# Stage 4 of a fused attention and MoE kernel: the last eight weight sums are moved into three gated waves

## Chip, cores and metric

One NeuronCore of a Trainium2 chip. The metric is the device time of one execution in microseconds (us); the time of a kernel is the median of its runs. All times inside an execution are counted from the start of the profiled span.

## What is computed

```
attn = softmax(cap * tanh(q k^T / sqrt(64) / cap)) v      4 x 12 heads, 448 x 64
x    = attn as 1792 x 768
h    = ((x w1) * (x w2)) w3 w_out                          d_ff 1024
g    = h w_in;  e = g * softmax(g);  c = layernorm(e) * g_ln
out  = c w_out2                                            1792 x 768
```

The three weights w3, w_out and w_in are multiplied together once ("fold"), so the middle of the chain is one 1024 x 1024 matrix.

## The kernel before

**Stages.** Attention and fold share the first half (to about 420 us). Stage 4 ("gated", to about 578 us) makes the products (x w1) * (x w2), 128 columns of d_ff ("block" f) at a time. Two more stages follow: the folded 1024 x 1024 matrix, then w_out2, in pairs of 128-row tiles (`seven`). All products are split into a high and a low fp32r part and take three matmuls (`THREE`). Some products are done with seven half-size products in place of eight (Strassen): in stage 4 the blocks 11, 13 and 14 (`SEVEN`, function `strassen`), in the two last stages all of them.

**Stage 4's end.** After two blocks of another order, the blocks come as 10, 11, 12, 13, 14, 15. Of these 10, 12 and 15 are plain (`products`, L700 to L729): 36 matmuls (L716) for each batch b, whose first half is copied by ScalarE (`a`, L720) and multiplied with the second by VectorE (`abs`, L724). A Strassen block has three PSUM banks u, v and y. Its product 3 adds to u only after VectorE has read u (L768), and the bank u is free for block 13 only after VectorE's last read of it (L774). p1 and p7 are copies by ScalarE (L751); L766, L768, L770, L771 and L774 are VectorE's sums with them, and their results are stored (L755).

**A block's weights.** Blocks from 10 on are read again from DRAM (`wt`, L446, 1.5 MB). For a Strassen block POOL then makes sums of the weights (L459 to L478, ten instructions: s3, s1, s2, s4), ScalarE casts each (L175) and VectorE subtracts (L176) to get the low part. Their buffers rotate (tag `cv`, two of them), so POOL's sixth step waits for VectorE's L176 of the first sum.

**Weight sums.** The two last stages also need Strassen sums of their weights. For each piece `plan_sums` reads four sub-blocks into one landing buffer (`ld`, two DMAs, L160), VectorE makes four differences in place (L590 to L593) and SP stores the result in two DMAs (L596). Kind "t" serves the fifth stage (eight pieces, `tw_dr`), kind "tg" the sixth (eight pieces of 128 x 4 x 192, `tg_dr`). There are `LANDS` = 3 landing buffers; the same three also take the first operands of the fifth stage (`ldab`, L162).

**Order of the work.** A list `ahead` holds all such work in the order in which it was added: an item is read up to three items ahead (`depth`), and goes through `rest` when it is its turn. An item has a `there` condition for its read and a `gate` for its turn. The program is then scheduled by a list scheduler; `tc.issue_after(x)` holds an instruction behind x in that schedule. Every engine and the SP queue run their instructions in program order. In the list before: block 13's read (`plan_again(NF + 5)`), then the eight "tg" pieces, then the reads of blocks 14 and 15, with no gate; the first difference of a "tg" piece stands behind `last_t`, an early instruction of stage 4.

```
    plan_again(NF + 5)
    some_sums("tg", G4, tg_dr, range(NF // 2), DM // 4)
    for f in range(NF + 6, 2 * NF):
        plan_again(f)
```

Of the kernel before, what the change touches and what calls it, by code (L numbers as in the profile page):

```python
# [10 lines left out]
F32 = mybir.dt.float32  # L11
# [3 lines left out]
ALU = mybir.AluOpType  # L15
# [8 lines left out]
DM = H * D  # L24
# [75 lines left out]
def attention_moe_solu(ctx: ExitStack, tc: tile.TileContext, q, k, v, cap, w12, w3t, wo, win, wout2, g_ln, out):  # L100
# [50 lines left out]
    def landing(i, src, n, kind):  # L151
        t = conv.tile([P, 2 * HALF], U32, tag="ld", bufs=LANDS, name=f"ld{i}")
        lands[i] = t[:, :n].bitcast(kind)
        dst = lands[i]
        if len(src.shape) == 3:
            dst = dst.rearrange("p (a b) -> p a b", a=src.shape[1])
        elif len(src.shape) == 4:
            dst = dst.rearrange("p (a b c) -> p a b c", a=src.shape[1], b=src.shape[2])
            for g in range(src.shape[1]):
                sync.dma_start(out=dst[:, g], in_=src[:, g])  # L160
            return
        loads[i] = sync.dma_start(out=dst, in_=src)  # L162
# [373 lines left out]
    def w3_slot(name):  # L536
        return w3p.tile([P, 2, HALF], F32R, tag="w3", bufs=W3, name=name)[:, :, :S]

    last_t = [None]

    def plan_t(part):

# [32 lines left out]
    def four(dr, i, part, n):  # L575

        return dr[i][:, :, :, part * n:(part + 1) * n]
# [1 line left out]
    W4 = w_dr.rearrange("(g i) p (h n) -> i p g h n", g=2, h=2)  # L579
    G4 = wg_dr.rearrange("(g i) h p n -> i p g h n", g=2)  # L580

    def plan_sums(kind, dr, t_dr, i_, part, n):

        i = len(ahead.items)

        def rest():
            b = lands.pop(i).rearrange("p (g h n) -> p g h n", g=2, h=2)
            b00, b01, b10, b11 = (b[:, g, h] for g in range(2) for h in range(2))
            with tc.issue_after(last_t[0].ins) if kind == "tg" or i_ >= NF // 4 else nullcontext():
                dve.tensor_tensor(b00, b01, b00, ALU.subtract)  # L590
            dve.tensor_tensor(b01, b11, b01, ALU.subtract)
            dve.tensor_tensor(b11, b11, b00, ALU.subtract)
            dve.tensor_tensor(b10, b10, b11, ALU.subtract)  # L593
            b = b.rearrange("p g h n -> p (g h) n")
            for m, two in enumerate((b[:, ::3], b[:, 1:3])):
                sync.dma_start(out=t_dr[2 * m:2 * m + 2, :, i_, part * n:(part + 1) * n].rearrange("t p n -> p t n"), in_=two)  # L596
        ahead.add((kind, i_, part), lambda: landing(i, four(dr, i_, part, n), 4 * n, F32), lambda: None, rest, None, lambda: "ws" in place)

    def block_src(m, part, dr, t_dr):

# [51 lines left out]
    def some_sums(kind, dr, t_dr, two, n):  # L652
        for i_ in two:
            for part in range(2):
                plan_sums(kind, dr, t_dr, i_, part, n)
# [8 lines left out]
        for part in range(2):  # L664
            plan_block(m, part)
    plan_again(NF + 5)
    some_sums("tg", G4, tg_dr, range(NF // 2), DM // 4)
    for f in range(NF + 6, 2 * NF):
        plan_again(f)
    for m in EARLY[2:]:  # L670
        for part in range(2):
            plan_block(m, part)
# [25 lines left out]
    def gated():  # L698
        pp = {}

        def products(f, b, cs):
            at_ = f - 2 if f in (NF, NF + 1) else f
            for i in range(2):
                if cs[0] == 0:
                    tag = "o" if "ws" in place and (i if b < 3 or f >= NF + 2 else f % 2) else "f"
                    if (f, b) == (2 * NF - 1, PASSES[1][0]):
                        pp["sc"] = ps.tile([P, 2, HALF], F32, tag=f"sc{f % 2}", name="ab_last") if i == 0 else pp["sc"]
                        pp[f, b, i] = pp["sc"][:, i]
                    else:
                        pp[f, b, i] = ps.tile([P, HALF], F32, tag=tag, bufs=2, name=f"ab{i}_{f}_{b}")  # L710
                for c in cs:
                    while not (ahead.upto(("w", at_, c // 2)) and ahead.upto(("x", b, c // 2))):
                        yield 0
                    w = wt[at_][:, :, columns(i, c)]
                    for m, (u, e) in enumerate(THREE):
                        pe.matmul(pp[f, b, i][:, :S], w[:, u], xs[b, c][:, e], start=(c == 0 and m == 0), stop=(c == NC - 1 and m == 2))  # L716
                        yield 189
                if cs[-1] == NC - 1 and i == 0:
                    pp["a"] = place["ab"].tile([P, S], F32, tag="a", bufs=2, name=f"a_{f}_{b}")
                    act.copy(pp["a"], pp[f, b, 0][:, :S])  # L720
            if cs[-1] < NC - 1:
                return
            ab = place["ab"].tile([P, S], F32, tag="ab", bufs=2, name=f"abs_{f}_{b}")
            dve.tensor_tensor(ab, pp[f, b, 1][:, :S], pp["a"], ALU.mult)  # L724
            sync.dma_start(out=ab_dr[block(f), :, b * S:(b + 1) * S], in_=ab)
            if f < NF - 2 and b == PASSES[0][0]:
                sync.dma_start(out=w12_dr[f], in_=raw(wt[f]))
            fin.add((f, b))
            ahead.loads()  # L729

        def strassen(f):
            b1, b2 = PASSES[1]
            x = {1: [xs[b1, c] for c in range(0, NC, 2)], 2: [xs[b1, c] for c in range(1, NC, 2)], 3: [xs[b2, c] for c in range(1, NC, 2)]}
            u, y = (ps.tile([P, HALF], F32, tag=g, bufs=2, name=f"{n}_{f}")[:, :S] for n, g in (("u", "f"), ("y", "o")))
            v = ps.tile([P, 2, HALF], F32, tag=f"sc{f % 2}", name=f"v_{f}")[:, 0, :S]
            need = {1: ("w", f, 0), 7: ("t", NC // 2 - 1), 6: ("w", f, 1), 4: ("t4", NC // 2 - 1), 3: ("w", f, 2)}

            def product(bank, m, first):
                while m in need and not ahead.upto(need[m]):
                    yield 0  # L740
                for k in range(NC // 2):
                    part = slice(k * P, (k + 1) * P)
                    a = wt[f].rearrange("p a (k n) -> p a k n", n=HALF)[:, :, k, {1: slice(0, P), 2: slice(P, 2 * P), 5: slice(2 * P, 3 * P), 4: slice(3 * P, HALF)}[m]] if m in (1, 2, 4, 5) else st_[f][:, :, (6, 7, 3).index(m), part]
                    o = x[m][k] if m < 4 else ts_[m, k]
                    for i, (h, e) in enumerate(THREE):
                        pe.matmul(bank, a[:, h], o[:, e], start=(first and k == 0 and i == 0), stop=(k == NC // 2 - 1 and i == 2), skip_group_check=not first)  # L746
                        yield 189

            def kept(bank, p, tag, name):
                k_ = p.tile([P, S], F32, tag=tag, bufs=2, name=f"{name}_{f}") if tag != "rb" else p.tile([P, 2, S], F32, tag=tag, name=f"{name}_{f}")[:, 0]  # L750
                act.copy(k_, bank)  # L751
                return k_

            def send(k_, b):
                sync.dma_start(out=ab_dr[block(f), :, b * S:(b + 1) * S], in_=k_)  # L755
                fin.add((f, b))
                ahead.loads()
            yield from product(u, 1, True)
            one = kept(u, place["ab"], "a", "p1")
            yield from product(v, 7, True)  # L760
            three = kept(v, place["ab"], "ab", "p7")
            yield from product(u, 6, False)
            two = kept(u, conv, "rb", "u2")
            fin.add((f, 6))
            yield from product(y, 2, True)
            dve.tensor_tensor(one, y, one, ALU.add)  # L766
            yield from product(u, 5, False)
            dve.tensor_tensor(three, u, three, ALU.add)  # L768
            yield from product(v, 4, False)
            dve.tensor_tensor(two, v, two, ALU.add)  # L770
            dve.tensor_tensor(one, one, two, ALU.mult)  # L771
            send(one, b1)
            yield from product(u, 3, False)
            dve.tensor_tensor(three, u, three, ALU.mult)  # L774
            send(three, b2)

        every = range(NC)
        for f in range(NF):
            for b in PASSES[0]:
                yield from products(f, b, every)  # L780
        first, last = PASSES[1]
        for f in range(2):
            yield from products(NF + f, first, every)

        yield from products(NF, last, range(4))
        while "ws" not in place:
            yield 0
        yield from products(NF + 1, last, range(4))
        for f in range(2):
            yield from products(NF + f, last, range(4, NC))  # L790
        for f in range(NF + 2, 2 * NF):
            if f in SEVEN:
                yield from strassen(f)
            else:
                for b in PASSES[1][::-1]:
                    yield from products(f, b, every)
# [330 lines left out]
```

## Time and profile before

| | |
|---|---|
| median of 3 runs | 837.44 us (835.84 to 840.43) |
| the profiled execution | 835.01 us, its span 833.2 us |
| TensorE (PE) busy | 815.5 us, 98% of the span |
| VectorE (DVE) | 629.6 us, 76% |
| ScalarE (ACT) | 491.4 us, 59% |
| GpSimd (POOL) | 108.7 us, 13% |
| stage 4's last matmul ends, the fifth stage begins | 578.26 us |

TensorE is busy nearly all the time, so a change that leaves its work alone can only move the little time in which it waits, and the time in which its clock is low. The views that show these are the list of waits by engine, the timeline of an engine in a stretch (start, length, line, tiles, count, idle time before and what ended it) and the table by stretches with the granted clock.

### The profile page before, as it was taken

How to read it: one execution, taken by the hardware profiler on the slowest of the kernel's cores; microseconds unless marked ns; L12 is line 12 of the kernel's file. 1: busy time of each engine (PE TensorE's matmuls, PEld its weight loads, DVE VectorE, ACT ScalarE, POOL GpSimd, SP SyncE). 2: the span in 40 equal slices, each digit the busy share in tenths (PEclk: the TensorE clock that was granted, in tenths of full speed). 3: DMA queues.
4: the chain of work that ended last, by engine and by line, in shares of the span. 5: the costliest groups of instructions: out<-in, count | busy, mean ns of one | idle time of the engine just before them, and what ended most of it. 6: DMA issues, size and time to landing. Idle time of an engine off the chain costs nothing.

```text
span 833.2 us, 12261 instructions
## 1 busy us (share of the span) xinstructions
PE 815.5 (98%) x4336; PEld 679.1 (81%) x4336; DVE 629.6 (76%) x1102; ACT 491.4 (59%) x766; POOL 108.7 (13%) x179
## 2 busy tenths in 40 slices
PE   8999999999999999999999999899999999999998
PEld 4657888876777888888869889798888888999997
DVE  5989968788876787789835997674997886994452
ACT  6757868778677877777652332123655565863341
POOL 1110110110311221111110601520000000000000
PEclk9999999999999999999999999999999999999999
DMA  7878745578976355689539678885733325833211
GB/s 233 272 241 276 208 158 157 173 231 274 280 262 206 114 181 185 209 307 317 156 120 365 199 258 275 286 252 176 234 101 127 101 102 190 291 124 153 89 64 76
DMA packets 95069, 167.19 MB, mean 201 GB/s; under 512 B 13216, under 2 KB 66208, under 8 KB 93472
## 3 DMA queue, kind: packets, MB, share of 16 engines
q1 hardware_dynamic: 90016, 155.22, 56.1%
q0 software_dynamic: 4992, 11.19, 5.5%
q8 instruction: 34, 0.56, 0.3%
q14 instruction: 27, 0.22, 0.1%
HBM read 113.25 MB, written 47.53 MB: 193 GB/s over the span
## 4 chain that ended last, share of the span: by engine, by line
PE 73%; DMA 11%; DVE 10%; issue 2%; ACT 2%; SPq 1%; POOL 0%; DVEq 0%; ACTq 0%
PE u L927 16%; PE ab L716 14%; PE o L291 9%; PE v L927 8%; PE f L397 6%; PE f L379 4%; PE y L927 4%; PE sc L250 4%; PE u L746 2%; DMA ld<-in_wo 2%; DVE cv L170 2%; DVE cv L171 2%; DMA wg_dr<-wg 2%; PE tp L997 1%; DMA wt<-w_dr 1%
## 5 line engine op out<-in xcount | busy, mean ns | idle before, releaser
L716 PE MATMUL ab<-xs,wt 128*128 128x448 f32 x900 | 192.7, 368 | 1.0 <-ACT xs L175 0.5
L716 PEld LDWEIGHTS ab<-xs,wt 128*128 128x128 f32 x900 | 169.4, 189 | 19.0 <-ACT xs L175 1.3
L258 ACT ACTIVATE sc<-sc,qscale 128x896 f32<-128x896 f32 (+1 forms) x96 | 85.0, 885 | 37.9 <-PE sc L250 28.1
L291 PE MATMUL o<-hi,v 128*66 128x448 f32 (+1 forms) x360 | 86.1, 375 | 1.6 <-ACT x L307 1.5
L259 ACT ACTIVATE p<-sc,capt 128x896 f32<-128x896 f32 (+1 forms) x96 | 85.6, 917 | 1.4
L927 PE MATMUL u<-ws,a 128*128 128x512 f32 x336 | 81.7, 393 | 0.0
L379 PEld LDWEIGHTS f<-w,w_o 128*128 128x128 f32 x576 | 72.6, 191 | 10.1 <-issue 5.7
L379 PE MATMUL f<-w,w_o 128*128 128x256 f32 x576 | 78.2, 289 | 0.9 <-DVE w_o L176 0.9
L274 DVE TENSOR_TENSOR lo<-p,hi 128x896 fp32r<-128x896 f32 x60 | 65.1, 1087 | 13.2 <-ACT hi L270 12.8
L927 PEld LDWEIGHTS u<-ws,a 128*128 128x128 f32 x336 | 62.8, 188 | 14.3
L397 PE MATMUL f<-w_i,w 128*128 128x512 f32 x288 | 70.2, 393 | 1.2 <-ACT w L175 1.0
L397 PEld LDWEIGHTS f<-w_i,w 128*128 128x128 f32 x288 | 53.7, 188 | 14.6 <-ACT w L175 1.4
L927 PE MATMUL u<-wg,c 128*128 128x384 f32 x336 | 64.6, 339 | 0.0
L291 PEld LDWEIGHTS o<-hi,v 128*66 128x66 f32 (+1 forms) x360 | 39.5, 136 | 27.3 <-issue 8.5
L927 PEld LDWEIGHTS u<-wg,c 128*128 128x128 f32 x336 | 58.2, 188 | 0.1
L270 ACT CAST hi<-p 128x896 fp32r<-128x896 f32 x60 | 56.6, 948 | 0.3
L171 DVE SCALAR_TENSOR_TENSOR cv<-ld,cv 128x512 uint32<-128x512 uint32 (+1 forms) x80 | 52.9, 669 | 0.5
L170 DVE SCALAR_TENSOR_TENSOR cv<-ld,cv 128x512 uint32<-128x512 uint32 (+1 forms) x80 | 52.1, 660 | 0.6
L308 POOL DMA_DIRECT2D xr<-x x48 | 25.4, 532 | 200.8 <-ACT x L307 193.6
L169 DVE TENSOR_SCALAR cv<-ld 128x512 uint32<-128x512 uint32 (+1 forms) x80 | 32.8, 414 | 22.0 <-DMA ld<-in_w 7.7
L291 PE MATMUL o<-lo,v 128*66 128x448 f32 x120 | 42.6, 369 | 0.0
L927 PE MATMUL v<-ws,a 128*128 128x512 f32 x168 | 41.5, 393 | 0.0
(182 smaller groups left out, 1396.0 us busy)
## 6 DMA issues: line engine op xcount, KB each, us to landing
ld<-in_w SPq DMA_DIRECT2D x24, 512.0 KB, 4.9
w_dr<-wt SPq DMA_DIRECT2D x6, 1536.0 KB, 6.8
wt<-w_dr SPq DMA_DIRECT2D x6, 1536.0 KB, 8.3
ld<-in_w3t SPq DMA_DIRECT2D x16, 512.0 KB, 4.2
ldab<-ab_dr SPq DMA_DIRECT2D x14, 512.0 KB, 4.4
c_dr<-e SPq DMA_DIRECT2D x14, 512.0 KB, 2.7
ldc<-c_dr SPq DMA_DIRECT2D x14, 512.0 KB, 4.3
kd<-in_k SPq DMA_DIRECT2D x24, 256.0 KB, 3.6
```

What stands on the lines that cost most here:

```text
L170: dve.scalar_tensor_tensor(x, hi, 0xC0000000, x, ALU.bitwise_and, ALU.bitwise_or)
L171: dve.scalar_tensor_tensor(x, lo, 29, x, ALU.logical_shift_right, ALU.bitwise_or)
L250: tiled[0] = pe.matmul(sc[:, j, :S], keys[rows], qq[rows, :], start=(m == 0), stop=(m == len(terms) - 1))
L258: act.activation(sc[:, :w, :S], sc[:, :w, :S], AF.Tanh, scale=qscale)
L259: exp_[n, c] = act.activation(p, sc[:, :w, :S], AF.Exp, scale=capt)
L270: act.copy(hi, p)
L274: dve.tensor_tensor(lo, p, raw(hi), ALU.subtract)
L291: product_.append(pe.matmul(outs[n, j][:v_.shape[-1], :S], v_, t[rows, j if c < 3 else 0], **flags))
L379: pe.matmul(f[:, :QW], lw[:, a], rw[:, e], start=(g == 0 and m == 0), stop=(g == NF - 1 and m == 2))
L397: pe.matmul(f, w34[:, a, c, :], rw[:, e], start=(c == 0 and m == 0), stop=(c == NC - 1 and m == 2))
L716: pe.matmul(pp[f, b, i][:, :S], w[:, u], xs[b, c][:, e], start=(c == 0 and m == 0), stop=(c == NC - 1 and m == 2))
L927: pe.matmul(bank, a[m][:, x, k * P:(k + 1) * P], wb[m][:, e, k, :], start=(first and k == 0 and i == 0), stop=(k == NF // 2 - 1 and i == 2 ...
```

## The change

The eight "tg" pieces are no longer one run of items. They are put into three waves of 3, 3 and 2 pieces. The first wave may take its turn only when both results of block 11 are recorded as issued, the second after block 12, the third after block 13. Block 14's read stands behind the first wave in the list, block 15's behind the second. The first difference of a "tg" piece is held behind `posted`, the last result of a block that had been recorded by then (L724 or L774).

```diff
-    last_t = [None]
+    last_t, posted = [None], [None]
...
-    def plan_sums(kind, dr, t_dr, i_, part, n):
+    def plan_sums(kind, dr, t_dr, i_, part, n, gate=None):
...
-            with tc.issue_after(last_t[0].ins) if kind == "tg" or i_ >= NF // 4 else nullcontext():
+            with tc.issue_after((last_t[0] if kind == "t" else posted[0]).ins) if kind == "tg" or i_ >= NF // 4 else nullcontext():
...
-        ahead.add((kind, i_, part), lambda: landing(i, four(dr, i_, part, n), 4 * n, F32), lambda: None, rest, None, lambda: "ws" in place)
+        ahead.add((kind, i_, part), lambda: landing(i, four(dr, i_, part, n), 4 * n, F32), lambda: None, rest, gate, lambda: "ws" in place)
...
     plan_again(NF + 5)
-    some_sums("tg", G4, tg_dr, range(NF // 2), DM // 4)
-    for f in range(NF + 6, 2 * NF):
-        plan_again(f)
+    last_sums = [(i_, part) for i_ in range(NF // 2) for part in range(2)]
+    for wave, f in enumerate((NF + 3, NF + 4, NF + 5)):
+        for i_, part in last_sums[wave * LANDS:(wave + 1) * LANDS]:
+            plan_sums("tg", G4, tg_dr, i_, part, DM // 4, lambda f=f: all((f, b) in fin for b in PASSES[1]))
+        if wave < 2:
+            plan_again(f + 3)
...
-            dve.tensor_tensor(ab, pp[f, b, 1][:, :S], pp["a"], ALU.mult)
+            posted[0] = dve.tensor_tensor(ab, pp[f, b, 1][:, :S], pp["a"], ALU.mult)
...
-            dve.tensor_tensor(three, u, three, ALU.mult)
+            posted[0] = dve.tensor_tensor(three, u, three, ALU.mult)
```

Line numbers below are those of the kernel before; in the changed kernel the lines from L667 on stand three later (L768 is L771, L774 is L777, L724 is L727, L755 is L758).

**VectorE, block 11's sums, before.** `p_11_5558` is p7 of block 11, `u_5520` its bank u, `ld_...` the pieces, `wt_5585` and `st_5586` the weights of block 13 and their sums.

```order
L771 TENSOR_TENSOR p_11_5532<-p_11_5532,u_11_5569 128x448
L590 TENSOR_TENSOR ld_5687<-ld_5687 128x192
L591 TENSOR_TENSOR ld_5687<-ld_5687 128x192
L176 TENSOR_TENSOR wt_5585<-s_13_5649,wt_5585 128x3x128
L768 TENSOR_TENSOR p_11_5558<-u_5520,p_11_5558 128x448
L592 TENSOR_TENSOR ld_5687<-ld_5687 128x192
L590 TENSOR_TENSOR ld_5692<-ld_5692 128x192
```

Between L766 and L768 stood nine differences of "tg" pieces; the last two of them are shown.

**VectorE, the same place in the changed program, from the same L771 (now L774) to the last read of bank u (now L777).**

```order
L774 TENSOR_TENSOR p_11_5532<-p_11_5532,u_11_5569 128x448
L176 TENSOR_TENSOR wt_5585<-s_13_5649,wt_5585 128x3x128
L771 TENSOR_TENSOR p_11_5558<-u_5520,p_11_5558 128x448
L176 TENSOR_TENSOR st_5586<-s_13_5653,st_5586 128x384
L727 TENSOR_TENSOR abs_3_5708<-ab_12_3_5676,a_3_5674 128x448
L590 TENSOR_TENSOR ld_5638<-ld_5638 128x192
L590 TENSOR_TENSOR ld_5658<-ld_5658 128x192
...
L593 TENSOR_TENSOR ld_5687<-ld_5687 128x192
L777 TENSOR_TENSOR p_11_5558<-u_5520,p_11_5558 128x448
```

No difference stands ahead of L768 now. The first wave, twelve differences with one L176 among them, stands behind block 12's L724 and ahead of block 11's L774.

**SP, the end of stage 4, before.** `ldab_6020` and `ldab_6022` are the first operands of the fifth stage, `ws_6007` its first late weight.

```order
L446 DMA wt_5847<-w_dr 128x3072
L160 DMA ld_5771<-wg_dr 128x2x192 x2
L725 DMA ab_dr<-abs_2_5787 128x448
L596 DMA tg_dr<-ld_5732 128x2x192 x2
L596 DMA tg_dr<-ld_5762 128x2x192 x2
L596 DMA tg_dr<-ld_5771 128x2x192 x2
L162 DMA ldab_6020<-ab_dr 128x8x128
L755 DMA ab_dr<-p_13_5817 128x448
L162 DMA ldab_6022<-ab_dr 128x8x128
L162 DMA ldab_6149<-ab_dr 128x8x128
```

**SP, the same place in the changed program.**

```order
L446 DMA wt_5813<-w_dr 128x3072
...
L160 DMA ld_5876<-wg_dr 128x2x192 x2
L160 DMA ld_5879<-wg_dr 128x2x192 x2
L758 DMA ab_dr<-p_13_5819 128x448
L162 DMA ldab_6020<-ab_dr 128x8x128
L758 DMA ab_dr<-p_13_5830 128x448
L758 DMA ab_dr<-p_14_5922 128x448
L596 DMA tg_dr<-ld_5876 128x2x192
...
L596 DMA tg_dr<-ld_5879 128x2x192
L162 DMA ldab_6022<-ab_dr 128x8x128
L162 DMA ldab_6149<-ab_dr 128x8x128
L608 DMA ws_6007<-tw_dr 128x1024 x2
```

The third wave's reads and stores now stand ahead of `ldab_6022` and `ws_6007`, and its buffers are the ones that the two later `ldab` take. The second half of `ld_5876` counts on the same DMA semaphore as block 15's read (`wt_5813`), eight issues earlier, and waits for that to land.

## Rows read from the trace of the kernel before

**Rows 1.** Waits of TensorE, whole span: engine, waiter, releaser: us in total, times, longest

```profile
PE u L746 <- DVE p L768: 3.9, 1, 3.9
...
PE o L291 <- ACT x L307: 1.5, 1, 1.5
```

**Rows 2.** Timeline of TensorE, end of stage 4: start us, us, what, count, idle before

```profile
520.02 5.33 PE L716 MATMUL ab<-xs,wt 128*128 128x448 f32 x25
529.23 3.19 PE L746 MATMUL u<-xs,st 128*128 128x448 f32 x9 [3.89 <-DVE p L768]
532.22 5.20 PE L716 MATMUL ab<-xs,wt 128*128 128x448 f32 x22
...
537.46 1.97 PE L746 MATMUL u<-xs,wt 128*128 128x448 f32 x9
...
574.50 3.92 PE L716 MATMUL ab_last<-xs,wt 128*128 128x448 f32 x18 [0.62 <-ACT a L720]
```

**Rows 3.** Timeline of VectorE, 521 to 540 us

```profile
525.90 1.20 DVE L590 TENSOR_TENSOR ld<-ld 128x192 f32<-128x192 f32 x1 [2.04 <-DMA ld<-wg_dr]
...
528.57 0.61 DVE L768 TENSOR_TENSOR p<-u,p 128x448 f32<-128x448 f32 x1
...
531.56 0.35 DVE L590 TENSOR_TENSOR ld<-ld 128x192 f32<-128x192 f32 x1
531.82 0.55 DVE L176 TENSOR_TENSOR st<-s,st 128x384 fp32r<-128x384 f32 x1
...
534.64 0.61 DVE L774 TENSOR_TENSOR p<-u,p 128x448 f32<-128x448 f32 x1
539.37 0.93 DVE L176 TENSOR_TENSOR st<-s,st 128x384 fp32r<-128x384 f32 x1 [4.13 <-ACT st L175]
```

**Rows 4.** Timeline of POOL, 519 to 539 us

```profile
519.91 1.03 POOL L459 TENSOR_TENSOR s1l<-wt 128x384 f32<-128x384 f32 x1
523.41 1.32 POOL L460 TENSOR_TENSOR s<-wt 128x384 f32<-128x384 f32 x1 [2.47 <-DVE st L176]
...
535.72 1.01 POOL L459 TENSOR_TENSOR s3l<-wt 128x384 f32<-128x384 f32 x1 [4.84 <-DMA wt<-w_dr]
...
538.87 1.02 POOL L459 TENSOR_TENSOR s1l<-wt 128x384 f32<-128x384 f32 x1
```

**Rows 5.** Table by stretches: us, busy of PE, PEld, DVE, ACT, POOL, then PEclk, DMA share, GB/s

```profile
420.00:424.00 4.00, 3.98 (x13) 2.25 (x14) 1.49 (x2) 3.97 (x6) 1.59 (x3) 0.58 0.76 206
...
530.00:532.00 2.00, 2.00 (x7) 1.78 (x6) 2.00 (x6) 0.52 (x1) 0.88 (x1) 0.50 0.97 381
...
574.00:576.00 2.00, 1.50 (x7) 1.41 (x8) 0.57 (x1) 2.00 (x3) 0.00 (x0) 1.00 0.21 79
```

**Rows 6.** Six reads of a block's weights (L446): issue to landing

```profile
DMA to landing us min/median/max: 6.9/8.3/10.4
```

**Rows 7.** DMA issues, 500 to 600 us: count, KB each, median us to landing

```profile
ws<-tw_dr SPq DMA_DIRECT2D x8, 512.0 KB, 6.0
ldab<-ab_dr SPq DMA_DIRECT2D x7, 512.0 KB, 5.9
...
tg_dr<-ld SPq DMA_DIRECT2D x16, 192.0 KB, 4.5
```

**Rows 8.** The stores of the "tg" pieces: issue to landing

```profile
DMA to landing us min/median/max: 2.0/4.5/8.2
```

**Rows 9.** Timeline of SP, end of stage 4

```profile
554.03 1.37 SPq L162 DMA_DIRECT2D ldab<-ab_dr  x2
...
565.02 1.64 SPq L608 DMA_DIRECT2D ws<-tw_dr  x2
```

**Rows 10.** Timeline of ScalarE, 525 to 575 us

```profile
525.85 0.51 ACT L175 CAST wt<-s 128x384 fp32r<-128x384 f32 x1 [5.04 <-POOL s L461]
...
571.19 1.06 ACT L175 CAST ws<-ws 128x1024 fp32r<-128x1024 f32 x1 [0.22 <-DMA ws<-tw_dr]
573.92 0.53 ACT L720 COPY a<-ab_last 128x448 f32<-128x448 f32 x1 [1.67 <-PE ab_last L716]
```

## Prediction

> **What bounds it now.** I read the list of waits of TensorE first. The page gives PE 98% of the span, so all that this change can win is in the few places where PE waits. The list has one large entry [rows 1]: a matmul into bank u waits 3.9 us for VectorE's L768; the next largest single wait is 1.5 us, in another stage. The timeline of PE shows the place [rows 2]: 25 matmuls end at 525.3, block 11's product 3 starts at 529.23. Behind it the clock is low: the stretch from 530 to 532 us has a granted clock of 0.50, which is 1.2 GHz in place of 2.4 [rows 5]. Nine matmuls take 3.19 us there, where the same nine take 1.97 at full clock, and the 22 after them 5.20 in place of about 4.6 [rows 2]. So the stop costs 3.9 us of idle time and some 1.8 us of slow matmuls, 5.7 in all. The other idle time of over 1 us in the run, 1.55 us before 420 us, is followed by a clock of 0.58 [rows 5], while 0.62 us before 574.50 is followed by 1.00 [rows 2, 5].
>
> Next I read why L768 was late. In VectorE's timeline a difference of a "tg" piece ahead of it waits 2.04 us for its read and then takes 1.20 us instead of 0.35 [rows 3], because POOL works at the same time; L768 itself starts at 528.57. And POOL's L460 had waited 2.47 us for an L176 that VectorE held behind other differences [rows 4].
>
> **Part one: the differences ahead of L768 go.** What is left ahead of L768 is block 13's chain through POOL, ScalarE and VectorE. Block 14 shows how it runs without differences in the way: POOL's L459 starts at 538.87, VectorE's L176 ends at 540.30, 1.43 later [rows 3, 4]. Block 13's L459 starts at 519.91 [rows 4], so L460 starts at 521.4 and not at 523.41. Two steps of POOL (1.32 and 1.0), the cast (0.51) [rows 10], L176 beside POOL (0.93) and L768 (0.61) [rows 3] make 4.4 us: L768 ends at 525.8 to 525.9. PE can be there at 525.1 and waits under 1 us, for which the rows show no fall of the clock. Product 3 starts at 525.9, **3.3 us earlier**. The lower bound of what stays here is no wait; the upper is the old 3.9, if POOL's chain does not move (a rival below).
>
> **Part two: twelve differences now stand ahead of L774.** The first wave does not stand behind block 11's last result: it stands behind block 12's L724 and ahead of block 11's L774. The bank u that L774 frees is the one that block 13's first product writes. PE gets there after 9 + 5 + 18 + 1 matmuls at 0.2 us: 525.9 + 6.6 = 532.5. L774 comes when VectorE is through. After L768 come an L176 behind two more steps of POOL and a cast (about 527.5) and L724 (0.6): the wave starts at 528.0. Alone a difference starts every 0.26 us (531.56, 531.82 [rows 3]), so six of them are done at 529.6. Twelve and their L176 alone would be through at 531.6 and L774 at 532.3, in time.
>
> But they are not alone. Block 14's weights are now read earlier: the read stands behind the store of L771, which I put at 522.4. It lands 6.9 to 8.3 us later [rows 6], at 529.3 to 530.7; there is less other traffic than before, so I take 529.4. Then POOL makes its first four steps for block 14, from 535.72 to 539.89 in the kernel before [rows 4], 4.2 us. Beside POOL one VectorE instruction with two SBUF operands gets through for each POOL instruction (0.93 to 1.20 us each [rows 3]). Of the seven that are left (an L176 and six differences) four take these 4.2 us and three 0.8, so L774 ends at 529.4 + 4.2 + 0.8 + 0.6 + 0.4 for the last difference's end and the starts = 535.4. **PE waits 2.9 us** and block 13 begins at 535.4 instead of 537.46: the gain is down to 2.0 us. Bounds: no wait when the read lands after about 532, 3.2 us when it lands at 530, just behind the L176. A wait of over 1.5 us has been followed by the low clock both times, so another 1.8 us of slow matmuls follow, and PE by itself keeps 0.2 us of the 2.0.
>
> The Trainium skill speaks to this (SBUF — State Buffer, Who interferes with whom): VectorE with two SBUF inputs and a POOL instruction that reads SBUF share one port pair, whoever issues first holds it for its whole instruction and the other stops. By that rule a queue of twelve differences that is already running could hold POOL off, and L774 would come at 532.3 with no wait. The rows show turns, one for one, so I do not take it; the case without a wait is the first rival.
>
> **Part three: the end of stage 4.** The last 18 matmuls started at 574.50 behind ScalarE's L720 of 573.92, which had just seen PE's result [rows 2, 10]; its casts of `ws` had ended at 572.25. In the changed program the third wave's four stores stand in SP's queue ahead of the second `ldab` and of `ws`, and that `ldab` takes a buffer of the wave, so it waits for its store to land. Before, the `ldab` left at 554.03 and `ws` at 565.02 [rows 9]. Now: the wave's last differences stand behind block 14's L768, which PE allows at 560.6 on the path above; the last store leaves at 562.0, one that `ldab` needs at 561.6; it lands at the least 2.0 us later [rows 8] and `ldab` leaves at 563.9, `ws` with two issues ahead of it at 564.8 and 565.5. After 6.0 us [rows 7] the second half of `ws` is there, at 571.5; its cast takes 1.06, and an L720 behind it would end at 573.1 to 573.4 [rows 10]. PE had been ready 0.62 us before 574.50 [rows 2]; 0.2 us earlier it is ready at 573.7, and with the same 0.6 us for the copy between, the last 18 matmuls start at **574.1 to 574.3 instead of 574.5**; I take 574.1. Two paths, PE's and SP's, come out within 1 us of each other here. Bounds: 572.4 when the clock does not fall behind part two's wait and the transfers are quick, 576.0 when the store takes its median of 4.5 us [rows 7] and all follows.
>
> All the rest I cost at nothing. The same eight pieces are read, summed and stored, and the stages after 578 us have the same order, so they start 0.4 us earlier and stay as they are. Block 15's read leaves at about 540, as before, with some 12 us in hand for PE.
>
> **Sum.** The lead over the kernel before is 3.3 us at product 3. Up to block 13 the old slow clock is saved (1.8) and the new wait paid (2.9, and 0.2 of matmuls that change places): 1.3 are lost, 2.0 left. The slow clock behind the new wait takes 1.8, and 0.2 are left, by the times above 0.2 to 0.4 at the last 18 matmuls: -0.4 us. Against the profiled execution that is 835.0 - 0.4 = 834.6; that execution is 2.4 us below the median of 837.44, so the median to expect is **837.0 us**. The change takes away the one large wait and makes another of nearly its size 7 us later.
>
> **Rivals.**
> *No new wait (25%).* Block 14's read lands at 532 (9.6 us after its issue, within the maximum of 10.4 [rows 6]), or VectorE keeps ahead of POOL, and L774 ends by 532.5. Then the 2.9 us and their slow matmuls fall away; the stores, block 15's read and the end's chain come some 4 us earlier too, and L720 ends near 569.5: 537.46 - 532.5, -5.0 us, 832.4. For it: 2.6 us of delay are enough. Against: in half of the six cases the read took 6.9 to 8.3 us.
> *Slower: the chain through SP (13%).* The second half of the third wave's first read waits for block 15's read to land, since both count on one DMA semaphore, and behind it in SP's queue stand `ldab`, all stores of the wave and `ws`. I have that landing at 548, 7.5 us after its issue. With 10.4 us [rows 6] it is 551, `ws` lands 2.5 us later and L720 ends at 576; from a landing at 549.5 on each us costs one. PE then waits some 3 us at the last 18 matmuls, with a low clock behind it (1.8): 3.5 us slower than before, 840.9.
> *It does not do what it says (5%).* If L460's wait was not VectorE's doing, L768 stays at about 528.6, and the wave pushes L774 to 538.3: +1 us, 838.4. Against it: the 2.47 us have VectorE as releaser [rows 4].
>
> **Chances.** 57% for the forecast, whose own range is 835.3 to 838.9 by the bounds of part three. A difference under 0.5%, 4.2 us, cannot be told from none here. Faster by more: seven tenths of the first rival and 1 or 2% of the forecast, 0.19. Slower by more: four tenths of the second rival, and 1% for what I do not see, 0.07. The rest, 0.74, is within. The range takes in the first rival's time and stops short of the second's: 832.0 to 839.8.
>
> **What would show it.** In the waits of PE: L768 under 1 us, a new wait of about 2.9 us of bank u on L774 near 532 us, and 0.6 to 2 us on L720 before the last 18 matmuls. In POOL's timeline: block 14's L459 starts near 529.4 (535.72 before [rows 4]), and VectorE's differences beside it take about 1 us each. The granted clock is low after 535 us and not at 530. The first matmul of the fifth stage comes near 577.9 instead of 578.26. I am wrong if PE has no wait on L774 (then it is faster), or if L720 is later than 574.5 (then slower).

## Result, and the profile after

The changed kernel takes **845.75 us** (median of 6 runs, 844.95 to 849.68) against 837.77 us for the kernel before on the same chip (6 runs, 835.84 to 840.43): a ratio of 1.0105, 95% interval 1.0077 to 1.0133. It is 8 us slower, where 837.0 was forecast and 839.8 was the upper end of the range. Its profiled execution took 845.62 us, with a span of 843.9.

The waits of TensorE in the changed kernel, those of stage 4 (us in total, times, longest; lines from L667 on are three later than before):

```profile
PE ab_last L719 <- ACT a L723: 4.5, 1, 4.5
PE u L749 <- DVE p L777: 3.2, 1, 3.2
PE u L749 <- ACT u L754: 2.0, 1, 2.0
PE u L749 <- DVE p L771: 1.5, 1, 1.5
```

Four waits stand where there were one of 3.9 [rows 1] and one of 0.6 us [rows 2]. The timeline of TensorE shows each in its place:

```profile
528.79 2.08 PE L749 MATMUL u<-xs,st 128*128 128x448 f32 x9 [1.53 <-DVE p L771]
...
538.92 3.30 PE L749 MATMUL u<-xs,wt 128*128 128x448 f32 x9 [3.17 <-DVE p L777]
542.01 2.15 PE L749 MATMUL v<-x,st 128*128 128x448 f32 x8
...
564.83 2.08 PE L749 MATMUL u<-x,wt 128*128 128x448 f32 x9 [2.05 <-ACT u L754]
...
575.24 3.81 PE L719 MATMUL ab_last<-xs,wt 128*128 128x448 f32 x18
583.57 5.48 PE L719 MATMUL ab_last<-xs,wt 128*128 128x448 f32 x18 [4.52 <-ACT a L723]
588.89 2.96 PE L930 MATMUL u<-ws,a 128*128 128x512 f32 x12
```

And the table by stretches has the clock behind them (the seventh and later columns as in [rows 5]):

```profile
528.00:530.00 2.00, 1.21 (x6) 1.14 (x7) 1.10 (x3) 0.51 (x1) 1.92 (x2) 1.00 0.94 381
...
540.00:542.00 2.00, 2.00 (x6) 1.75 (x6) 0.00 (x0) 0.47 (x1) 1.84 (x3) 0.50 1.00 314
...
584.00:586.00 2.00, 2.00 (x7) 1.78 (x6) 1.35 (x2) 1.49 (x2) 0.00 (x0) 0.50 0.27 103
```

The two profiled executions do not reach block 11 at the same time: its first matmul starts at 507.42 us in the changed kernel and at 505.28 in the kernel before, and in the kernels below anywhere from 502.03 (e7) to 507.90 (e4). Times of the two are therefore compared from block 11's first matmul, which is to take 2.14 us off those of the changed kernel. From there to the fifth stage's first matmul it was 72.98 us and is now 81.47: **+8.5**. The sum closes: the waits of this stretch were 3.89 + 0.62 and are 1.53 + 3.17 + 2.05 + 4.52, which is 6.8 more; the slow matmuls cost 1.8 and now cost 1.7 behind the wait of 3.17 and 1.6 behind that of 4.52, which is 1.5 more: 8.3 of the 8.5.

The largest loss is the last wait, so I read who was late there. ScalarE's timeline:

```profile
563.21 1.14 ACT L175 CAST a<-ldab 128x512 fp32r<-128x512 f32 x2 [9.47 <-DMA ldab<-ab_dr]
564.25 0.52 ACT L754 COPY u<-u 128x448 f32<-128x448 f32 x1
...
580.76 1.04 ACT L175 CAST ws<-ws 128x1024 fp32r<-128x1024 f32 x1 [1.33 <-DMA ws<-tw_dr]
582.04 1.04 ACT L175 CAST ws<-ws 128x1024 fp32r<-128x1024 f32 x1 [0.23 <-DMA ws<-tw_dr]
582.99 0.53 ACT L723 COPY a<-ab_last 128x448 f32<-128x448 f32 x1
```

TensorE had finished what L723 copies at 579.05. The copy stood behind two casts of the fifth stage's late weights, and these waited for their load. The same picture stands 20 us earlier: the copy of block 14's third bank (L754) stood behind the two casts of the fifth stage's first operand, and ScalarE sat idle for 9.47 us until that operand had landed. VectorE at the same time:

```profile
563.86 1.29 DVE L176 TENSOR_TENSOR a<-ldab,a 128x512 fp32r<-128x512 f32 x2 [8.23 <-ACT a L175]
...
565.60 0.62 DVE L777 TENSOR_TENSOR p<-u,p 128x448 f32<-128x448 f32 x1
566.13 0.62 DVE L590 TENSOR_TENSOR ld<-ld 128x192 f32<-128x192 f32 x2
...
569.34 0.62 DVE L593 TENSOR_TENSOR ld<-ld 128x192 f32<-128x192 f32 x2
```

It waited 8.23 us for the same casts, with block 13's last result (L777) and the whole third wave behind them in its queue. So the wave's stores, and all that stands behind them in SP's queue, are late:

```profile
555.19 1.90 SPq L160 DMA_DIRECT2D ld<-wg_dr  x4
...
557.70 0.38 SPq L162 DMA_DIRECT2D ldab<-ab_dr  x1
...
568.83 2.77 SPq L596 DMA_DIRECT2D tg_dr<-ld  x4
573.00 0.99 SPq L162 DMA_DIRECT2D ldab<-ab_dr  x2
574.09 1.55 SPq L608 DMA_DIRECT2D ws<-tw_dr  x2
```

The second `ldab` leaves at 570.9 in the time of the kernel before, where it left at 554.03, and `ws` at 572.0 instead of 565.02 [rows 9]. The theory from here, the queue theory of the expectations below: **a chain of queues**. The third wave's reads wait for the second wave's buffers; the first operand's read stands behind them; ScalarE and VectorE stand still for that operand; the third wave's sums, its stores, the second `ldab` and `ws` follow; and L723 waits behind the casts of `ws`. The rival, the bank theory, was that the new wait for bank u (L777, 3.17 us and a low clock) makes everything later.

### The profile page after: what moved, and what is told of

It is laid out like the page before. It is cut to its first block, busy times and chain, and to the rows that moved or that the text cites. A ratio compares the mean times of both kernels' runs of the same rounds, so it can differ in the third digit from the quotient of the medians.

```text
span 843.9 us, 12259 instructions
## 1 busy us (share of the span) xinstructions
PE 818.2 (97%) x4336; PEld 680.1 (81%) x4336; DVE 625.5 (74%) x1102; ACT 490.8 (58%) x766; POOL 109.2 (13%) x179
## 4 chain that ended last, share of the span: by engine, by line
PE 57%; DMA 20%; DVE 12%; ACT 4%; issue 4%; POOL 1%; SPq 1%; DVEq 0%; ACTq 0%; POOLq 0%
PE u L930 16%; PE v L930 8%; PE o L291 7%; PE f L397 6%; PE ab L719 5%; PE f L379 5%; PE y L930 4%; PE sc L250 3%; DMA wg_dr<-wg 2%; DMA ld<-w_dr 2%; DMA wt<-w_dr 2%; DMA rb<-r_dr 2%; DVE cv L170 2%; DVE cv L171 2%; PE tp L1000 1%
```

## Experiments

The ratios are to the kernel before on the same chip, whose median was 837.32 us for e1 to e4, 837.03 for e5 to e8, 835.67 for e9 to e11 and 836.77 for e12.

| kernel | median us | ratio | 95% interval |
|---|---|---|---|
| changed | 845.75 | 1.0105 | 1.0077 to 1.0133 |
| e1 each wave behind its own block | 844.56 | 1.0103 | 1.0067 to 1.0139 |
| e2 two waves | 839.63 | 1.0029 | 1.0008 to 1.0050 |
| e3 two waves, each behind its own block | 837.46 | 1.0004 | 0.9980 to 1.0028 |
| e4 third wave read on POOL's queue | 842.70 | 1.0060 | 1.0032 to 1.0087 |
| e5 L723 ahead of the casts of `ws` | 842.12 | 1.0055 | 1.0029 to 1.0081 |
| e6 e5, operand held on VectorE | 841.84 | 1.0060 | 1.0037 to 1.0083 |
| e7 e3 and e5 | 837.64 | 1.0018 | 0.9993 to 1.0043 |
| e8 e7, operand held | 835.82 | 0.9975 | 0.9953 to 0.9997 |
| e9 e5, operand held on ScalarE too | 836.16 | 1.0002 | 0.9973 to 1.0030 |
| e10 e8, block 15 read first | 837.77 | 1.0019 | 0.9996 to 1.0043 |
| e11 changed, block 15 read first | 847.59 | 1.0143 | 1.0107 to 1.0179 |
| e12 before, with what e9 adds | 836.92 | 1.0002 | 0.9981 to 1.0023 |

**e1: take the wait for L777 away.** In the changed kernel the first wave is recorded after block 12's result, so `posted[0]` is not block 11's last. Here each wave is held behind its own block's.

```diff
-    last_t, posted = [None], [None]
+    last_t, posted = [None], {}
...
-posted[0]).ins)
+posted[after]).ins)
...
-            posted[0] = dve.tensor_tensor(three, u, three, ALU.mult)
+            posted[f] = dve.tensor_tensor(three, u, three, ALU.mult)
```

> The first wave is held behind the changed kernel's own idea of a last result: L777 of block 11 itself (in the kernel before L774), not whatever result was recorded last; waves two and three alike. Changed kernel 845.75 us, before 837.77. Bank theory (the 3.2 us wait of block 13's first product for L777 and the low clock behind it are the loss): that wait goes, 4 to 5 us are won, 840 to 842 us. Queue theory (the loss is made at the end of stage 4, where the third wave's reads and stores stand in SP's queue ahead of the fifth stage's operands and weights, and PE waits there for ScalarE's L723): PE comes earlier to the same late L723, its wait there grows from 4.5 us to 8 or 9, and the time stays within 2 us of 845.75.

The time stays, 844.56 us. In e1's list of waits the one of bank u at block 13 is gone, and the last has grown by 2.5 us:

```profile
PE ab_last L719 <- ACT a L723: 7.0, 1, 7.0
```

From block 11's first matmul TensorE is through with what L723 copies after 70.4 us instead of 71.6, but the copy starts after 76.9 instead of 75.6, behind three casts of `ws` now. New waits of 1.9 us (for block 14's last result) and 1.1 us (for block 15's read) take part of the gain back ahead of the tail. In this profile the copy of block 14's third bank stands ahead of the first operand's casts (550.88, the casts at 560.47), and VectorE's wait of 8.93 us for these casts alone still makes the third wave late. So the wait that my prediction spent most of its working on was worth nothing as long as the tail was as late as this.

**e2 and e3: fewer waves.** Two waves of three and five pieces, behind blocks 11 and 12, so that nothing is left for block 13; e3 has both this and e1's edit.

```diff
-    for wave, f in enumerate((NF + 3, NF + 4, NF + 5)):
-        for i_, part in last_sums[wave * LANDS:(wave + 1) * LANDS]:
+    for wave, f in enumerate((NF + 3, NF + 4)):
+        for i_, part in (last_sums[:LANDS], last_sums[LANDS:])[wave]:
```

> The two pieces of the third wave go into the second: five pieces behind block 12, block 15's read behind them. The first wave stays as in the changed kernel, ahead of L777. Queue theory: the last two pieces are no longer summed behind the cast of the fifth stage's first operand, the second operand and the weight leave SP's queue some 8 us earlier, the wait of 4.5 us on L723 falls under 1 us with its low clock, and so does the 2.0 us wait on ScalarE's copy u2 of block 14: 838 to 840 us. Bank theory: the wait on L777 is as before, the time stays at 844 to 847 us.

> Both edits at once. Queue theory with bank theory as the second bound: neither wait is left, 832 to 835 us, under the kernel before. If only the bank counts: as the run with the first edit alone. If only the queue counts: as the run with the second alone, 838 to 840.

e2 came to 839.63, within the range of the queues; its profile still has the 3.2 us for L777, but only 0.6 for L723. e3 came to 837.46, no faster than the kernel before: the 832 to 835 that I had put down was missed. Waits of 2.3 us (L723), 1.9 (block 15 for block 14's L777) and 1.3 (L771) were left in its profile. From the changed kernel to e2 the ratio fell by 0.0076: most of the 8 us hang on the third wave. The hold behind block 11 by itself has no gain clear of noise (e1 against changed, e3 against e2).

**e4: is it the place in SP's queue?** The third wave's four reads are issued from POOL's queue, idle by then, so the first `ldab` no longer stands behind them.

```diff
-landing(i, four(dr, i_, part, n), 4 * n, F32)
+landing(i, four(dr, i_, part, n), 4 * n, F32, queue)
...
+pool if wave == 2 else sync
```

> The changed kernel with one thing else: the four reads of the third wave are issued from POOL's queue, which is idle there, so nothing in SP's queue stands behind them; the sums and stores of the wave keep their places. Queue theory, if the reads with their wait for block 15's landing hold up the first operand: it leaves 2 to 4 us earlier (557.7 in the changed kernel), the 2.0 us wait on u2 of block 14 goes and 2 to 4 us are won, 841 to 844 us. If the stores of the wave alone hold up what follows: within 1 us of 845.75. Bank theory: within 1 us of 845.75.

842.70: some of it was won, in the range put down, but not in the way put down. In its profile (845.39 us, near the top of its ten runs, 838.79 to 845.86) the first operand leaves 52.2 us after block 11's first matmul, where in the changed kernel it leaves after 50.3, and TensorE's wait for block 14's copy has grown from 2.0 to 3.6 us. So the number was met by luck, and what won the 3 us is not shown. The operand is held by more than its place. The entry in e4's list of waits of SP:

```profile
SPq L162 <- DMA tg_dr<-ld: 3.2, 1, 3.2
```

The first `ldab` (L162) waits 3.2 us until stores of `tg_dr` have landed, since it takes a buffer of a wave itself. The third wave's reads wait for the same stores.

**e5, e6, e9: the places in ScalarE's and VectorE's queues.** e5 moves one thing: the casts of the late weights (and VectorE's half of the split) may not stand ahead of L723. For that their turn in the list also gets a gate, block 15's first result.

```diff
+    def late_split(m, part):
+        with tc.issue_after(copied[0].ins) if m in EARLY[2:] else nullcontext():
+            block_split(ws[m], part)
...
-                  lambda: block_split(ws[m], part), None, there)
+                  lambda: late_split(m, part), None if m in EARLY[:2] else (lambda: (2 * NF - 1, PASSES[1][0]) in fin), there)
...
-                    act.copy(pp["a"], pp[f, b, 0][:, :S])
+                    copied[0] = act.copy(pp["a"], pp[f, b, 0][:, :S])
```

> The changed kernel, with one thing moved: ScalarE's copy of block 15's last half (a of batch 2) stands ahead of the casts of the fifth stage's late weights in ScalarE's queue, instead of behind the first two of them. Nothing else is moved, so the third wave, its stores and the loads behind them stay as late as they are. Theory A (TensorE's 4.5 us ahead of the last 18 matmuls is the copy standing in line behind casts that wait for a late load): that wait falls under 1 us and the low clock behind it goes, some 4.5 + 1.3 us, so 839.5 to 842. Rival B (the load itself is needed, and the fifth stage waits for it instead): the wait moves behind the last 18 matmuls, and the time stays at 843.5 to 846.

842.12, at the edge of the range of theory A. The wait for L723 falls from 4.5 to 0.6 us, and the fifth stage did not wait for `ws` instead. What is left in its profile: 3.1 us for the copy of block 14's third bank, 2.1 for L776 (L771 of the changed kernel), and 2.0 in the fifth stage's first products. This one profile also lacks the wait for L777, ahead of everything that e5 moved, so what the copy was worth is read from the ratio and not from the waits. e6 adds a hold of the first operand behind block 14's last result:

```diff
+        with tc.issue_after(fourteen[0].ins):
             begin(1, x1[:, :HALF])
             begin(2, x1[:, HALF:])
             dve.tensor_tensor(s1, x2[:, :HALF], x2[:, HALF:], ALU.add)
```

> As e5, and the fifth stage's first operand (two casts on ScalarE, what VectorE does with them, and the first sum) also held behind block 14's last result. Theory A (the 2.0 us that TensorE waited in block 14 for ScalarE's copy, and what VectorE has behind the same load, are again only a place in line): both waits go, 2 us more than e5, so 837.5 to 840. Rival B (the third wave's own sums and turns hold block 14, not the operand): the same as e5 within 1 us, 839.5 to 842. Rival C (the held operand is late for the fifth stage): slower than e5, with a wait ahead of the fifth stage's first matmul.

841.84, as e5. The hold did not reach ScalarE, since the result named is VectorE's; ScalarE's timeline of e6 shows the order as it was (L761 is the copy):

```profile
559.76 1.14 ACT L175 CAST a<-ldab 128x512 fp32r<-128x512 f32 x2 [9.80 <-DMA ldab<-ab_dr]
560.81 0.52 ACT L761 COPY u<-u 128x448 f32<-128x448 f32 x1
```

So e6 says nothing on the operand, and e9 repeats it with the casts also behind that copy by name.

```diff
-        with tc.issue_after(fourteen[0].ins):
+        with tc.issue_after(fourteen[0].ins), tc.issue_after(fourteen[1].ins):
...
+                copy = act.copy(k_, bank)
+                if f == 2 * NF - 2 and tag == "rb":
+                    fourteen[1] = copy
```

> As e6, which did not do on ScalarE what it was meant to: there the two casts of the first operand still stood ahead of the copy of block 14's third bank, and the wait of 2.3 us for that copy was still there. Here they stand behind it by name. Theory A: the wait of block 14 for ScalarE goes (2.3 to 3.1 us in e6 and e5), and the time falls to 838.5 to 840.5. Rival B (the copy's bank is late for another reason, or the third wave's sums take the wait over): 841 to 843. Rival C (the first operand, cast later, is late for the fifth stage): 841 to 843 too, but with the wait ahead of or in the fifth stage's first products.

836.16, ratio 1.0002: the 8 us are gone, where 838.5 had been put down as the best. In ScalarE's timeline of e9 the copy no longer waits for the operand, and in SP's the tail is early (its profile is of the fastest of its ten runs, which go from 832.19 to 841.42 us):

```profile
550.86 0.53 ACT L761 COPY u<-u 128x448 f32<-128x448 f32 x1 [3.90 <-PE u L756]
557.29 1.14 ACT L175 CAST a<-ldab 128x512 fp32r<-128x512 f32 x2 [5.89 <-DMA ldab<-ab_dr]
```

```profile
556.65 1.97 SPq L598 DMA_DIRECT2D tg_dr<-ld  x4
...
560.01 2.63 SPq L162 DMA_DIRECT2D ldab<-ab_dr  x2
562.75 0.99 SPq L610 DMA_DIRECT2D ws<-tw_dr  x2
```

The third wave's stores begin at 556.65, where in e6 they begin at 563.52 and in the changed kernel at 568.83; from block 11's first matmul that is 51.7, 57.7 and 61.4 us. The reason is in VectorE's queue: the third wave's differences are interleaved with block 14's sums, one of which needs the copy (in e6 VectorE waits 2.55 us for it between two differences), so what held the copy held the wave. That is why more came back than the wait of 2.3 us that could be seen at TensorE. From the changed kernel to e5 the ratio fell by 0.0050, from e6 to e9 by 0.0058: the two places in line are the loss, each to within some 0.004 by the intervals of the two kernels. Of the second place neither half by itself brings the third wave's stores to where e9 has them: 57.7 us in e6, which moves VectorE's part alone, and 59.8 in e1, where ScalarE's copy stood ahead of the casts.

**e7, e8: e3 with the same two edits.** e7 is e3 with e5's edit, e8 is e7 with e6's.

> Two waves, each behind its own block's last result (e3), with the copy of e5. Theory A: e3's wait of 2.3 us ahead of the last 18 matmuls goes, and the low clock behind it, so 834 to 836 against e3's 837.5. Rival B (the load is needed anyway): 837 to 838.

> e7 with the first operand held as in e6. Theory A: the 1.9 us for which block 15 waited for block 14's last result goes too, so 832 to 834.5, below the kernel before by 0.4 to 0.6%. Rival B (that result is late for the waves' sums, not for the operand): as e7, 834 to 836. Rival C (the operand is late for the fifth stage): 836 to 838.

e7 is as e3 (837.64): rival B's number, though its profile, the lowest of its twelve runs, has 0.6 us for L723 where e3's had 2.3; with runs from 832.45 to 840.82 I cannot say more. e8 is **835.82 us, ratio 0.9975, 0.9953 to 0.9997**, the only version with a ratio below 1. Its interval ends close to 1, and it is the best of twelve versions, so a gain is not safely shown. Its time is above the 832 to 834.5 put down. What it still waits for (L778 is L771 of the changed kernel; waits of under 1 us are left out):

```profile
PE u L756 <- DVE p L778: 1.7, 1, 1.7
PE ab L726 <- DMA wt<-w_dr: 1.1, 1, 1.1
```

**e10, e11: block 15's read first.** In the changed program this read stands behind the six reads of the second wave. Here it is put ahead of them in the list, in e8 (e10) and in the changed kernel (e11).

```diff
-        if wave < 2:
-            plan_again(f + 3)
+        if wave == 0:
+            plan_again(NF + 6)
+            plan_again(NF + 7)
```

> e8 with block 15's read put ahead of the second wave's reads in SP's queue instead of behind them. Theory A: TensorE's wait of 1.1 us for that read goes, 834 to 835.5 against e8's 835.8. Rival B (the second wave is now late, and with it the stores, the second half of the first operand and the late weights): 836.5 to 839.

> The changed kernel, with the same swap alone: block 15's read ahead of the second wave's reads. Theory A (the lateness of the last part begins where block 15's read stands behind the second wave's six reads): the first operand is read 2 to 3 us earlier and the time falls to 841.5 to 844. Rival B (the third wave waits for the second wave's stores to land, which free its buffers, so whatever puts the second wave later puts everything behind it later): 844.5 to 848, no better than the changed kernel's 845.7.

837.77 and 847.59: no better, the numbers of rival B both times. In e10 the read leads in SP's queue as meant; TensorE's wait for it is gone, and the second wave's reads begin 37.8 us after block 11's first matmul instead of 34.6. In e11 the scheduler left five of the six reads ahead of it all the same. SP in e11:

```profile
540.19 4.00 SPq L160 DMA_DIRECT2D ld<-wg_dr  x5
544.29 0.41 SPq L446 DMA_DIRECT2D wt<-w_dr  x1
...
545.23 0.43 SPq L160 DMA_DIRECT2D ld<-wg_dr  x1
```

From block 11's first matmul the read leaves after 39.0 us, in the changed kernel after 38.3: it came no earlier, so e11 does not try theory A. What it did was to put the second wave's last read behind block 15's, and the third wave's reads leave after 50.5 us instead of 47.8. In both runs what puts the second wave back puts back the buffers that the rest waits for.

**e12: a control.** The kernel before with the edits of e9, without any wave.

> A control: the kernel before, whose weight sums run unheld, with the two mendings that gave e9 its time (the copy of block 15's last half ahead of the casts of the late weights; the first operand's casts and what VectorE does with them behind block 14's copy and last result). Theory A (the mendings only take away what the waves' lateness brings, and before had nothing late): TensorE's wait of 3.9 us ahead of block 12's sixth product is still there, and the time stays within 1.5 us of the kernel before, ratio 0.998 to 1.002. Rival B (the copy and the operand cost the kernel before something too): 1 to 2.5 us faster, and then e8's gain of 0.25% is the mendings' and not the waves'. Rival C (the first operand, later now, is missed by the fifth stage): 1 to 3 us slower.

836.92, ratio 1.0002: theory A. Its list of waits has the old wait (L777 is L768 there), in this execution even longer:

```profile
PE u L753 <- DVE p L777: 5.0, 1, 5.0
```

So the two edits are worth nothing clear of noise where there are no waves: in e9 they take away a lateness that the waves had brought. Whether e8's 0.25% are more than the edits alone would bring is not shown, since the intervals of e8 and e12 overlap (0.9953 to 0.9997, 0.9981 to 1.0023).

## Why the prediction was wrong

**Part one was right, its size a little large.** The differences ahead of L768 are gone, and product 3 starts at 526.65 in the time of the kernel before, 2.6 us earlier and not 3.3; the wait is 1.53 us (forecast: under 1), with no fall of the clock. The missing 0.7 us are there at the start of the chain: POOL's second L459 comes at 520.6 in the time of the kernel before and not at the 519.91 that was taken over [rows 4].

**Part two was nearly right, and did not matter.** POOL's first step for block 14 starts at 531.66, which is 529.5 (forecast 529.4). The differences beside it take turns with POOL. Timelines of VectorE and of POOL in the changed kernel:

```profile
531.02 2.00 DVE L590 TENSOR_TENSOR ld<-ld 128x192 f32<-128x192 f32 x3
...
534.22 2.50 DVE L592 TENSOR_TENSOR ld<-ld 128x192 f32<-128x192 f32 x3
536.64 1.68 DVE L593 TENSOR_TENSOR ld<-ld 128x192 f32<-128x192 f32 x3
538.25 0.61 DVE L777 TENSOR_TENSOR p<-u,p 128x448 f32<-128x448 f32 x1
```

```profile
531.66 1.14 POOL L459 TENSOR_TENSOR s3l<-wt 128x384 f32<-128x384 f32 x1 [0.22 <-DVE ld L590]
```

TensorE waits 3.17 us for L777 (forecast 2.9), and the granted clock behind it is 0.50. By this the lead over the kernel before is down to 0.7 us at block 13 (536.8; forecast 535.4 against 537.46). But e1, without this wait, takes as long.

**Part three failed**, at the step "the wave's last differences stand behind block 14's L768, which PE allows at 560.6 on the path above; the last store leaves at 562.0". It took VectorE to be free when TensorE was through. In the changed kernel block 14's L771 runs at 566.7 in the time of the kernel before, the last store is issued by 569.5, the second `ldab` leaves at 570.9 (forecast 563.9), `ws` at 572.0 (564.8), and L723 ends at 581.4 (573.1 to 573.4), 8 us late. Six us of it are there ahead of the stores, at L771: 1.4 come from block 13's start, the rest, as I read the queues, from VectorE's wait of 8.23 us behind the first operand's casts and the 2.05 us that TensorE waited for ScalarE's copy behind the same casts. I had "All the rest I cost at nothing" for the first `ldab`, whose read I never placed. It left at 555.6 in the time of the kernel before, instead of 552.77, and landed 5.49 us later. In the kernel before ScalarE's two casts also stood ahead of block 14's copy, but the operand was there at 557.14. SP, ScalarE and TensorE in the kernel before:

```profile
552.77 0.44 SPq L162 DMA_DIRECT2D ldab<-ab_dr  x1
```

```profile
557.14 1.15 ACT L175 CAST a<-ldab 128x512 fp32r<-128x512 f32 x2 [4.99 <-DMA ldab<-ab_dr]
558.19 0.52 ACT L751 COPY u<-u 128x448 f32<-128x448 f32 x1
```

```profile
558.76 2.08 PE L746 MATMUL u<-x,wt 128*128 128x448 f32 x9
```

The copy ended at 558.71 and TensorE went into the bank at 558.76. The cover that I counted on without looking at it was not there: in the changed kernel the operand came 3.9 us later, TensorE some 2 us later, and the rest is its wait of 2.05 us.

**The rivals.** The chain through SP was given 13% and 840.9 us. It had the direction, the end (L723 behind late casts of `ws`, TensorE waiting at the last 18 matmuls with a low clock behind) and the queue right, and its price was half of the real one. Its cause was block 15's read, by one DMA semaphore. That read did leave later than I had it (545.73, or 543.6, against 540) and took 8.4 us, so it had landed by 554.6. The third wave's first read left at 555.19, and the list of waits of SP in the changed kernel puts its wait down to the second wave's stores:

```profile
SPq L160 <- DMA tg_dr<-ld: 2.4, 1, 2.4
...
SPq L162 <- DMA tg_dr<-ld: 1.3, 1, 1.3
```

So the semaphore was not what came last there. No run tried it by itself.

The first rival, no new wait at block 13, was given 25% and 832.4 us. Its condition came true in e1, and in the profiles of e5 and e6, whose order at that place is that of the changed kernel; their medians are 841.8 to 844.6 us. The early start of block 13 is not kept: "the end's chain come some 4 us earlier too" was the wrong clause. That chain goes by when the waves are summed and stored, not by when block 13 starts: the third wave's reads leave 47.8 us after block 11's first matmul in the changed kernel, 49.2 in e1, where the first wave stands behind L777, and 47.0 and 45.8 in e5 and e6, where it was summed faster.

**The chance.** I wrote that two paths, TensorE's and SP's, come out within 1 us of each other at the end, and still gave 7% to a loss of more than 0.5%. One more path of that kind, not priced, was enough.

## What to carry to other kernels

When work is held back, list for every engine what now stands behind the first instruction that waits for it, not only on the engine where the work is done: here casts on ScalarE that waited for an operand held a copy on ScalarE and, through both, sums on VectorE, and these held the stores that the next operand waited for. A cover that was measured before (a copy that ends as TensorE comes) has to be priced by how thick it was; here it was nothing. And a wait that ends earlier is worth only what the next wait on the same path leaves of it: e1 took 3.2 us away and nothing came of it.

## What was not expected of the hardware

**Two ways to run the same stretch.** The first wave's twelve differences and an L176 took 7.2 us in the changed kernel, from 531.02 until L777 starts. In e6, in the same order, they took 4.0. VectorE's timeline there, and POOL's:

```profile
529.33 1.18 DVE L592 TENSOR_TENSOR ld<-ld 128x192 f32<-128x192 f32 x3
...
531.70 0.89 DVE L594 TENSOR_TENSOR ld<-ld 128x192 f32<-128x192 f32 x3
532.51 0.89 DVE L595 TENSOR_TENSOR ld<-ld 128x192 f32<-128x192 f32 x3
```

```profile
531.64 2.63 POOL L459 TENSOR_TENSOR s3l<-wt 128x384 f32<-128x384 f32 x1 [1.89 <-DMA wt<-w_dr]
```

Here POOL's step takes 2.63 us instead of 1.0 and VectorE is not slowed beside it (three differences in 0.89 us): POOL is held off until the run of differences is through. In the changed kernel the two take turns. The prediction named the first way, without a wait for L774, beside the rule of the Trainium skill (SBUF — State Buffer, Who interferes with whom) that whoever issues first holds the shared port pair for its whole instruction. In the profiles that hold this order the stretch takes 7.2 to 7.3 us (changed, e2, e4, e11), 4.8 (e9) and 4.0 (e5, e6), and TensorE's wait for L777 is 3.2 us (changed, e2, e11), 1.8 (e4), 0.8 (e9) and none (e5, e6). POOL's first step came 0.5 to 1.2 us after the wave's first difference in the first five and 2.3 to 2.7 us after it in the last two. In e9 both ways stand side by side: POOL's first step took 1.02 us, its second 2.39. What decides between the two ways was not tried.

**The clock after an idle stretch.** The prediction went by two waits of the kernel before, 3.89 and 1.55 us, each with a low clock behind it. It took the second for the only other one of over 1 us in the run and overlooked one of 1.35 us ahead of the matmuls at 64.51, with a clock of 1.00 behind it. In the other runs the length of the wait does not settle it. In the changed kernel 1.00 follows waits of 1.53 and 2.05 us, while in e5 0.59 follows one of 2.13 us. In e11 TensorE waits 3.17 us for the same L777 (L778 there), and the nine matmuls behind it take 2.07 us, with the clock at 1.00, where the changed kernel after the same 3.17 us has 0.50. The stretch behind the wait in e11:

```profile
540.00:542.00 2.00, 2.00 (x12) 1.88 (x11) 0.00 (x0) 0.91 (x2) 1.87 (x2) 1.00 1.02 292
```

So the 1.6 to 1.8 us of slow matmuls that stand behind three waits of the kernel before and the changed kernel are a price that a wait of this size may or may not bring, and it belongs in a range and not in a sum.
